# Attention and two expert layers on one core: the 1e-9 of the softmax sums added by a reduction over pairs instead of by a scalar addition

## Chip, cores and metric

The kernel runs on one core of a Trainium2 chip, as one launch. The metric is device microseconds of the whole execution, the median of the runs that were made of a kernel; lower is better.

## The reference

Three layers follow each other. The first is attention over 2 batches x 8 heads x 768 positions x 64 features, with a mask: every query and every key is assigned to the centroid (16 per head) that it is most similar to, and a query sees only keys of its own centroid.

```python
scores = np.where(mask, scale * np.matmul(q, k.transpose(0, 1, 3, 2)), -1e9)
attn = np.exp(scores - np.max(scores, axis=-1, keepdims=True))
attn = attn / (np.sum(attn, axis=-1, keepdims=True) + 1e-09)
out = np.matmul(attn, v)
```

The 1e-9 of the third line is what the change is about. The 1536 x 512 result then goes through a layer `s * relu(x @ w_in)**2 + b` times `w_out` (512 to 2048 to 512), and through eight experts of width 1024, whose gates are softmax values normalised eight times over rows and columns. All of it is float32.

## The kernel before

Float32 precision is had by splitting each float32 operand of a matrix product into a high part and a remainder (`hh`/`hl`, `ath`/`atl`, `xh`/`xl`, `wh`/`wl`) and multiplying the pairs of parts on TensorE.

**Attention** (the first fifth of the span) goes over 96 query tiles `g` (16 heads x 6 tiles of 128 queries); three tiles make a `half` (32 of them). For each tile TensorE makes 128 x 768 scores (`score`, L422), VectorE takes the negated row maximum from PSUM (`row_max`, `m`, L428), ScalarE takes the exponential and sums the row on the way (`expo`, L435, `accum_out` into one column of `sums`), TensorE transposes the result (`transp`, L450), ScalarE takes the transposed tile out of PSUM as `ath` (L457) and VectorE writes the remainder `atl` (L463), which frees the PSUM tile for the next transposes. TensorE then multiplies by the values (`values`, L473) while the next half is being made. Once per half VectorE adds 1e-9 to the three sums (`rsum`, L480) and takes their reciprocals (L481); TensorE broadcasts these over partitions (`rb_rows`, L487), ScalarE copies them out (`rs`, L497) and the output halves `xb`, `xt` (L499, L504), and GpSimd adds (L505) and scales (L506) the output into `x1`.

Other work is spread over the tiles by hand-written plans: the preparation of the next heads (`prepare`, `norms`), and, from tile 74 on, the first units of weights of the second layer. These are unpacked from words: ScalarE (L567, L569), VectorE (`bits`, L576, L578, L580), GpSimd (`join`, L587, L588), then a split into `wh` on ScalarE (L598) and `wl` on GpSimd (L600).

In attention the order of each engine's instructions is not that of the code alone: the framework orders them by priorities and its own estimates of time. The expert layers are inside `manual_schedule()`, where the order is that of the code. They begin with `x_parts(0)` on VectorE: four times a copy (L624) and a subtraction (L625), and TensorE's first products (L120) need these. The tiles `xh`, `xl` take the memory of attention's tiles, so the first L624 waits for the last L473. After that the rest of the span is one matrix product after another, with VectorE, ScalarE and GpSimd preparing the operands.

Of the kernel before, what the change touches and what calls it, by code (L numbers as in the profile page):

```python
# [8 lines left out]
F32 = mybir.dt.float32  # L9
# [5 lines left out]
AX = mybir.AxisListType  # L15
PSUM = bass.MemoryType.PSUM

P = 128
# [35 lines left out]
class Kernel:  # L54
# [69 lines left out]
    def constants(self):  # L124
        nc, per = self.nc, self.per
        cst = per.tile([P, 2 * P + 1], F32, name="cst")
        nc.sync.dma_start(cst, self.cst_in)
        self.ident, self.floor = cst[:, :P], cst[:, 2 * P : 2 * P + 1]

        self.band = per.tile([P, P], BF16, name="band")  # L130
        nc.vector.tensor_copy(self.band, cst[:, P : 2 * P])
# [209 lines left out]
    def attention(self):  # L341
        nc = self.nc
# [70 lines left out]
        sc, ex, sums, aT, pv = {}, {}, {}, {}, {}  # L413
# [16 lines left out]
        def expo(g):  # L430
            half, i3 = divmod(g, 3)
            if i3 == 0:
                sums[half] = self.tile("sums", [P, 3], bufs=3)
            e = ex[g] = self.tile("e", [P, S], bufs=2)
            nc.scalar.activation(  # L435
                e.rearrange("p (u k) -> p u k", u=2), sc.pop(g)[:, :, :HALF], AF.Exp,
                bias=sc.pop((g, "m")), accum_out=sums[half][:, i3 : i3 + 1],
            )

        def transp(g):  # L440
# [35 lines left out]
                    )  # L476

        def rsum(half):
            r = sums[half]
            nc.vector.tensor_scalar_add(r, r, 1e-9)  # L480
            nc.vector.reciprocal(r, r)  # L481

        def rb_rows(half):
            r = sums.pop(half)
            rb = pv[half, "rb"] = self.ps("t", [D, 512])
            for i in range(3):
                nc.tensor.transpose(  # L487
                    rb[:, i * P : i * P + P], r[:, i : i + 1].to_broadcast([P, D]), self.ident
                )
# [23 lines left out]
        row_max(0)  # L513
        score(1)
        expo(0)
        row_max(1)
        score(2)
        for g in range(n_tiles + 4):
            live = g < n_tiles
            if g + 2 < n_tiles:  # L520
                row_max(g + 2)
            if g + 1 < n_tiles:
                expo(g + 1)
            done = g // 3 - 1
            if g % 3 == 0 and done > 0:
                finish(done - 1)
            if live:
                ts = transp(g)
            if g + 3 < n_tiles:
                score(g + 3)  # L530
            if live:
                evac_hi(g, ts)
            if done >= 0 and g < n_tiles + 3:
                if g % 3 == 0:
                    rsum(done)
                values(done, g % 3)
                if g % 3 == 2:
                    rb_rows(done)
            for st in plan.get(g, ()):
                st[0](*st[1:])  # L540
            if live:
                evac_lo(g, ts)
            if g == 71:
                self.weights_follow()
                for u in range(3):
                    self.load_unit(u)
# [540 lines left out]
```

## Time and profile before

| | us |
|---|---|
| median of 3 runs | 1611.36 |
| lowest, highest | 1610.91, 1613.38 |
| profiled execution, device time | 1610.82 |
| its span, first to last instruction | 1609.0 |
| TensorE / VectorE / GpSimd / ScalarE busy | 1544.8 / 1009.2 / 892.3 / 766.4 |

The span is what the profile shows of the execution; 1.8 us of the device time lie around it. An engine that is busy with an instruction may be waiting inside it: the profile counts from the start of the instruction to its end. Times in the views count from the start of the span.

### The profile page before, as it was taken

To read this page: it belongs to the slowest core of one execution; us is meant where nothing else is said; L and a number is where in the kernel's file an instruction comes from. 1 tells how busy PE (TensorE), PEld (TensorE's weight loads), DVE (VectorE), ACT (ScalarE), POOL (GpSimd) and SP (SyncE) were. 2 spreads that over 40 slices of the span, in tenths; PEclk is the share of its full clock that TensorE was granted. 3 is DMA by queue.
4 is the path that set the end of the run, shared out by engine and by line. 5 is a ranking of instruction groups with operands and counts; after the bars stand their busy time and mean duration, and the time that the engine had idled before them with its cause. 6 is when DMAs were issued, how large, how long until landed. Compare 5 with 4: busy or idle time off the path is not lost.

```text
span 1609.0 us, 21766 instructions
## 1 busy us (share of the span) xinstructions
PE 1544.8 (96%) x8136; PEld 1402.2 (87%) x8136; DVE 1009.2 (63%) x1594; ACT 766.4 (48%) x1432; POOL 892.3 (55%) x650
## 2 busy tenths in 40 slices
PE   4899998799999999999999999999999999999998
PEld 3778996699999988889989988998899889889987
DVE  7999999787788475545445545565455455455454
ACT  4789899576656553343333333333343333333331
POOL 5664446423233556556666575668657565665652
PEclk7999999899999999999999999999999999999999
DMA  9774451112111002112112121213212121221211
GB/s 259 184 181 112 102 148 53 53 53 79 53 53 53 1 27 79 53 53 79 61 70 79 53 79 53 79 58 113 79 53 79 53 79 56 76 79 53 79 53 40
DMA packets 26793, 124.69 MB, mean 77 GB/s; under 512 B 4448, under 2 KB 4576, under 8 KB 16448
## 3 DMA queue, kind: packets, MB, share of 16 engines
q1 hardware_dynamic: 26112, 120.95, 23.5%
q0 software_dynamic: 576, 2.36, 0.7%
q8 instruction: 64, 1.05, 0.3%
q14 instruction: 41, 0.34, 0.1%
HBM read 99.80 MB, written 3.15 MB: 64 GB/s over the span
## 4 chain that ended last, share of the span: by engine, by line
PE 81%; DVE 9%; ACT 4%; issue 2%; DMA 2%; POOL 1%; SPq 0%; DVEq 0%; ACTq 0%; POOLq 0%
PE t L120 33%; PE s L938 22%; PE y L938 11%; PE s L664 6%; PE pv L473 3%; PE u L120 2%; PE s L422 2%; DVE atl L463 2%; DVE m L428 2%; PE t L450 1%; DVE sums L480 1%; ACT e L435 1%; DVE hl L650 1%; DVE c L852 1%; PE u L450 1%
## 5 line engine op out<-in xcount | busy, mean ns | idle before, releaser
L917 ACT ACTIVATE hh<-c 128x384 fp32r<-128x384 f32 x256 | 134.6, 526 | 619.7 <-PE y L938 250.2
L845 POOL TENSOR_TENSOR wl<-raw,wh 128x1024 fp32r<-128x1024 f32 x64 | 154.1, 2408 | 359.1 <-ACT wh L844 359.1
L918 DVE SCALAR_TENSOR_TENSOR hl<-c,hh 128x384 fp32r<-128x384 f32 x256 | 211.9, 829 | 170.9 <-ACT hh L917 170.9
L938 PE MATMUL s<-wh,hl 128*128 128x512 f32 x512 | 202.5, 396 | 0.0
L938 PE MATMUL s<-wl,hh 128*128 128x512 f32 x512 | 201.8, 394 | 0.0
L938 PE MATMUL s<-wh,hh 128*128 128x512 f32 x512 | 200.9, 392 | 0.0
L120 PE MATMUL t<-th,ah 128*128 128x384 f32 x512 | 173.2, 338 | 4.5 <-ACT c L977 1.9
L120 PE MATMUL t<-th,al 128*128 128x384 f32 x512 | 172.3, 337 | 0.0
L120 PE MATMUL t<-tl,ah 128*128 128x384 f32 x512 | 171.9, 336 | 0.0
L837 POOL TENSOR_TENSOR al<-sm,ah 128x1024 fp32r<-128x1024 f32 x64 | 165.7, 2589 | 4.9 <-ACT ah L834 4.9
L120 PE MATMUL t<-xh,ah 128*128 128x384 f32 x384 | 130.3, 339 | 0.1
L835 POOL TENSOR_TENSOR al<-raw,ah 128x768 fp32r<-128x768 f32 x64 | 129.7, 2027 | 0.0
L120 PE MATMUL t<-xh,al 128*128 128x384 f32 x384 | 129.7, 338 | 0.0
L120 PE MATMUL t<-xl,ah 128*128 128x384 f32 x384 | 129.3, 337 | 0.0
L988 DVE TENSOR_TENSOR c<-t,c 128x384 f32<-128x384 f32 x64 | 35.7, 558 | 142.8 <-PE t L120 142.8
L587 POOL TENSOR_TENSOR fa<-fa,wraw 128x1024 f32<-128x1024 f32 x16 | 39.1, 2445 | 148.9 <-ACT r L646 108.0
L938 PEld LDWEIGHTS s<-wh,hl 128*128 128x128 f32 x512 | 96.0, 187 | 22.1
L938 PEld LDWEIGHTS s<-wh,hh 128*128 128x128 f32 x512 | 96.1, 188 | 11.9
L938 PEld LDWEIGHTS s<-wl,hh 128*128 128x128 f32 x512 | 96.0, 188 | 11.8
L120 PEld LDWEIGHTS t<-th,ah 128*128 128x128 f32 x512 | 96.1, 188 | 10.2 <-ACT c L977 2.8
L938 PE MATMUL y<-wh,hl 128*128 128x512 f32 x256 | 100.8, 394 | 0.0
L938 PE MATMUL y<-wl,hh 128*128 128x512 f32 x256 | 100.7, 393 | 0.0
(219 smaller groups left out, 4067.9 us busy)
## 6 DMA issues: line engine op xcount, KB each, us to landing
raw<-in_w SPq DMA_DIRECT2D x64, 1024.0 KB, 4.8
wraw<-in_w SPq DMA_DIRECT2D x16, 1024.0 KB, 4.8
raw<-in_qk SPq DMA_DIRECT2D x16, 384.0 KB, 4.5
ka<-hi SPq DMA_DIRECT2D x28, 192.0 KB, 3.7
nat<-in_qkn SPq DMA_DIRECT2D x6, 768.0 KB, 6.5
vraw<-in_v SPq DMA_DIRECT2D x8, 384.0 KB, 4.8
out<-x SPq DMA_DIRECT2D x12, 256.0 KB, 2.1
qa<-hi SPq DMA_DIRECT2D x14, 192.0 KB, 2.6
```

The costliest lines, as they stand in the source:

```text
L120: self.nc.tensor.matmul(out, a, b, start=(i == 0), stop=(i == n - 1))
L422: nc.tensor.matmul(s[:, u, :HALF], a[:, qs], k[:, u * HALF : u * HALF + HALF], start=(a is qa), stop=(a is qb))
L473: nc.tensor.matmul(o, vt[:, kt].rearrange("p a d -> p (a d)"), aT[half][w][:, kt, :], start=(kt == 0 and w == 0), stop=(kt == QT - 1 and w ...
L587: nc.gpsimd.tensor_tensor(a, a, raw[:, :, 0].bitcast(F32), op=ALU.mult)
L664: nc.tensor.matmul(o, a, b, start=(start and i == 0), stop=(stop and i == 2))
L835: nc.gpsimd.tensor_tensor(al[:, : 3 * Q], raw[:, : 3 * Q], f32(ah[:, : 3 * Q]), op=ALU.subtract)
L837: nc.gpsimd.tensor_tensor(al[:, 3 * Q :], self.sums.rearrange("p a b -> p (a b)"), f32(ah[:, 3 * Q :]), op=ALU.subtract)
L845: nc.gpsimd.tensor_tensor(wl, raw[:, 1024:], f32(wh), op=ALU.subtract)
L917: nc.scalar.activation(hh, c, AF.Relu)
L918: nc.vector.scalar_tensor_tensor(hl, c, 0.0, f32(hh), op0=ALU.max, op1=ALU.subtract)
L938: nc.tensor.matmul(ys[t][m], a, b, start=(start and i == 0), stop=(stop and i == 2))
L988: nc.vector.tensor_tensor(p1, ta, p1, op=ALU.add)
```

## The change

Three tiles of [128, 3, 2] are made once and filled with 1e-9. ScalarE's running sums go into element 0 of each pair. In `rsum` a sum over the pairs (a TENSOR_REDUCE) takes the place of the addition of a constant (a TENSOR_SCALAR), and writes to a tile of its own, `rsum`, in which the reciprocal is then taken. The tile `sums`, of which there were three in turn, is gone.

```diff
         cst = per.tile([P, 2 * P + 1], F32, name="cst")
         nc.sync.dma_start(cst, self.cst_in)
         self.ident, self.floor = cst[:, :P], cst[:, 2 * P : 2 * P + 1]
+
+        self.sums3 = [per.tile([P, 3, 2], F32, name=f"sums{i}") for i in range(3)]
+        for t in self.sums3:
+            nc.vector.memset(t, 1e-9)
...
             if i3 == 0:
-                sums[half] = self.tile("sums", [P, 3], bufs=3)
+                sums[half] = self.sums3[half % 3]
...
-                bias=sc.pop((g, "m")), accum_out=sums[half][:, i3 : i3 + 1],
+                bias=sc.pop((g, "m")), accum_out=sums[half][:, i3, :1],
...
         def rsum(half):
-            r = sums[half]
-            nc.vector.tensor_scalar_add(r, r, 1e-9)
+            r = self.tile("rsum", [P, 3], bufs=2)
+            nc.vector.reduce_sum(r, sums[half], axis=AX.X)
             nc.vector.reciprocal(r, r)
+            sums[half] = r
```

## Rows read from the trace of the kernel before

**Rows 1.** The page's chain that ended last, shares of the span by engine.
```profile
PE 81%; DVE 9%; ACT 4%; issue 2%; DMA 2%; POOL 1%; SPq 0%; DVEq 0%; ACTq 0%; POOLq 0%
```
**Rows 2.** Stretches: length, each engine's busy time (instructions), clock, DMA share, GB/s.
```profile
core 0: us, PE busy (x) PEld busy (x) DVE busy (x) ACT busy (x) POOL busy (x), PEclk, DMA share, GB/s
...
294.00:301.00 7.00, 0.14 (x2) 0.07 (x2) 6.97 (x4) 1.53 (x4) 7.00 (x4) 0.70 0.42 150
301.00:307.00 6.00, 6.00 (x22) 5.55 (x22) 2.23 (x6) 1.43 (x4) 1.15 (x2) 0.50 0.00 0
307.00:312.00 5.00, 3.56 (x14) 2.23 (x14) 4.04 (x7) 0.99 (x3) 2.33 (x2) 1.00 0.00 0
312.00:400.00 88.00, 87.01 (x496) 86.60 (x496) 67.55 (x84) 62.24 (x112) 24.97 (x10) 1.00 0.17 58
```
**Rows 3.** TensorE's waits, 250 to 316 us: us in total, times, longest.
```profile
PE t L450 <- DVE atl L463: 13.7, 7, 6.9
```
**Rows 4.** The source view of line 480: ns minimum/median/maximum.
```profile
L480 DVE TENSOR_SCALAR sums<-sums x32: 147/160/6723, 45.4 to 293.5; 128x3 f32<-128x3 f32 x32
```
**Rows 5.** VectorE's groups of the whole span: busy us, mean ns | idle before.
```profile
L428 DVE TENSOR_REDUCE m<-s 128x1 f32<-128x768 f32 x96 | 90.8, 946 | 4.4 <-PE s L422 3.9
...
L480 DVE TENSOR_SCALAR sums<-sums 128x3 f32<-128x3 f32 x32 | 21.1, 658 | 1.4 <-ACT e L435 1.4
...
L212 DVE TENSOR_REDUCE rn<-nat 128x24 f32<-128x1536 f32 x4 | 7.0, 1738 | 1.1 <-ACT nat L197 1.1
...
L741 DVE TENSOR_REDUCE t<-pm 128x12 f32<-128x96 f32 x8 | 2.0, 252 | 0.0
```
**Rows 6.** Timeline of VectorE, 250 to 305 us: start, duration, instruction.
```profile
260.42 1.78 DVE L480 TENSOR_SCALAR sums<-sums 128x3 f32<-128x3 f32 x1
262.12 0.68 DVE L580 TENSOR_SCALAR fa<-ft 128x1024 uint32<-128x1024 uint32 x1
...
264.58 1.51 DVE L480 TENSOR_SCALAR sums<-sums 128x3 f32<-128x3 f32 x1
...
267.99 2.14 DVE L576 TENSOR_SCALAR ft<-fa 128x1024 uint32<-128x1024 uint32 x1
...
293.50 6.72 DVE L480 TENSOR_SCALAR sums<-sums 128x3 f32<-128x3 f32 x1 [1.19 <-ACT e L435]
```
**Rows 7.** Timeline of GpSimd, 250 to 305 us.
```profile
259.82 2.36 POOL L600 TENSOR_TENSOR wl<-ft,wh 128x1024 fp32r<-128x1024 f32 x1 [3.99 <-ACT wh L598]
...
266.14 1.00 POOL L506 TENSOR_TENSOR x<-xb,rs 64x384 f32<-64x384 f32 x1
...
293.22 2.38 POOL L587 TENSOR_TENSOR fa<-fa,wraw 128x1024 f32<-128x1024 f32 x1
...
297.86 2.33 POOL L588 TENSOR_TENSOR ft<-ft,fa 128x1024 f32<-128x1024 f32 x1
300.16 0.99 POOL L505 TENSOR_TENSOR xb<-xb,xt 64x384 f32<-64x384 f32 x1
```
**Rows 8.** Timeline of GpSimd, 620 to 640 us.
```profile
619.61 2.40 POOL L845 TENSOR_TENSOR wl<-raw,wh 128x1024 fp32r<-128x1024 f32 x1 [8.20 <-ACT wh L844]
```
**Rows 9.** Timeline of VectorE, the same stretch.
```profile
621.32 0.25 DVE L741 TENSOR_REDUCE t<-pm 128x12 f32<-128x96 f32 x1
```
**Rows 10.** Timeline of TensorE, 124 to 132 us.
```profile
129.50 0.55 PE L450 MATMUL t<-cst,e 128*128 128x128 f32 x3 [0.24 <-DVE atl L463]
```
**Rows 11.** ScalarE's waits, 250 to 296 us.
```profile
ACT ath L457 <- PE t L450: 3.6, 5, 1.0
```
**Rows 12.** The chain that ended last, 300 to 311 us, in order of time.
```profile
302.48 3.53 PE pv L473 x11
...
306.04 0.37 DVE xh L624
...
308.23 1.24 DVE xl L625
309.48 1.08 DVE xh L624
```
**Rows 13.** Timeline of VectorE at the kernel's start.
```profile
4.95 0.56 DVE L241 TENSOR_SCALAR raw<-raw 128x768 f32<-128x768 f32 x1 [1.31 <-DMA raw<-in_qk]
```

## The prediction

> **What bounds the kernel now.** I read the chain first. TensorE holds most of it, VectorE 9% [rows 1]. The table of stretches then says where TensorE is not full. From 312 us on it is busy 87 of 88 us [rows 2], and no wait there has to do with softmax, so the change can act on the expert layers only by letting them start earlier: whatever attention gains by its end, the whole time gains. From 294 to 301 us, on the other hand, TensorE is busy 0.14 us of 7, VectorE 6.97 and GpSimd all 7 [rows 2]. TensorE's list of waits names the reason: its transposes wait for VectorE's `atl`, 13.7 us between 250 and 316 us, and one of these waits is 6.9 us long [rows 3].
>
> The source view of L480 explains that wait. The addition takes 0.16 us in the median, but 6.72 us once [rows 4]. Its 32 executions sum to 21.1 us [rows 5], where 32 x 0.16 would be 5.1: 16.0 us of it are not work. Laid beside GpSimd's timeline, each long execution ends when a GpSimd instruction does: the one of 260.42 at 262.20, with L600's end at 262.18; the one of 293.50 at 300.22, with L588's at 300.19 [rows 6, 7]. VectorE is held by GpSimd inside this instruction. In the last case it is held through three GpSimd instructions in a row, from L587 at 293.22 to the end of L588 [rows 7], although two of them ended on the way.
>
> **What the change removes.** Does a TENSOR_REDUCE also wait for GpSimd? The nearest row is L741, a sum with source and destination in SBUF: 0.25 us from 621.32, while GpSimd's L845 ran from 619.61 to 622.01 [rows 8, 9]; it began and ended inside L845, at the mean of its eight [rows 5]. So I take it that the reduction does not wait. The Trainium skill says the same of this chip (SBUF — State Buffer, Who interferes with whom): an addition of a constant can use a port pair that VectorE shares with GpSimd, `tensor_reduce` never does.
>
> **What it adds.** Its own duration: 252 ns for 96 elements (L741) and 1738 ns for 1536 (L212) [rows 5] make 1.03 ns an element, so 6 elements cost 252 - 90 x 1.03 = 159 ns, the addition's median. Bounds: 147 ns, the shortest addition [rows 4], and L741's 252 ns, 0.09 more; six of the 32 lie where VectorE sets the pace (from 250 us), so 0.6 us at most. I take 159 and no difference. The three memsets run before VectorE idles 1.31 us for a load [rows 13]; even at 0.16 us each they are hidden, and without that cover they would cost 0.5 us. ScalarE writes the same sums at another step; no wait is added for it, because a tile of pairs comes back three halves later.
>
> **What of the 16.0 us lies on the path.** I go through the long executions.
>
> - Twelve executions are longer than 0.2 us. The six of them before 250 us hold 4.5 us of the stalls. TensorE is nearly full there. The longest of these (1.4 us, ending at 128.8) makes TensorE wait 0.24 us behind the `atl` that follows it [rows 10]. I take 0.2 us for all six; bounds 0 and 2.0 (1.2 if the whole of this one counts, and 0.8 at 45 us, where the chain names a DMA and not L480).
> - 260.42: the next VectorE instruction but for the reciprocal is L580, a TENSOR_SCALAR too, which then itself waits for L600 until 262.18 [rows 6, 7]. It ends where it ended. The same holds at 252, 281 and 285 us (L576, L576 and L578 come next). Gain 0.1, taken as 0.
> - 264.58: this one gains. It ends 1.35 us earlier, L576 (267.99) then comes at 266.6 and waits for L506 until 267.14 [rows 6, 7] instead of for L588, and ends at 267.7 in place of 270.13: 2.4 us earlier. But ScalarE stands in the same loop, and all it can give up from 250 to 296 us is 3.6 us of waits for TensorE's transposes, five of at most 1.0 [rows 11]; some 1.8 of these come by 276 us. I take 1.7, near that limit, because GpSimd's next instruction waits for ScalarE; bounds 0 and 2.4.
> - 293.50: without the stall, and with TensorE's clock still at 1.00 for the last L473s (11 in 3.53 us while 0.50 was granted, 1.2 of 2.4 GHz; at 1.00 the half of that, 1.8 us less [rows 2, 12]), L624 comes 6.56 + 1.8 = 8.3 us earlier, near 297.7 instead of 306.04.
>
> **Where the last stall goes.** L624 and L625 run with both operands in SBUF, and they wait for GpSimd too: L625 at 308.23 took 1.24 and L624 at 309.48 another 1.08 [rows 12]. At 297.7 GpSimd is still in its row of three. L624 will sit there until 300.19 [rows 7], as L480 did, and 2.4 us of the 8.3 are given back: 5.9 left. After that GpSimd has four more instructions of 1.0 us (L505 and L506 of the last two halves), of which two met the eight instructions before. All four may now alternate with them, or none: 5.9 - 2.1 = 3.8, or 5.9 + 1.5 = 7.4. I keep 5.9. Last the clock: it fell in the idle stretch of 294 to 301 us (mean 0.70), stood at 0.50 to 307 and was back at 1.00 [rows 2]. TensorE will now idle some 3 us and be half idle after that; a fall would cost at most the half of a stretch of 6 us, 3.0, and nothing where TensorE waits anyway. I take 1.0. So this place gives 4.9 us, with bounds 3.8 - 3.0 = 0.8 and 8.3 + 1.5 = 9.8.
>
> **The sum.** 0.2 + 1.7 + 4.9 = 6.8 us. The profiled execution had 1610.8 us, 0.5 below the median, so 1604.0 on it and 1604.5 for the median. Of the 16.0 us of stalls less than half comes back. The bounds add to 0.8 - 0.6 = 0.2 (1611.2) and 2.0 + 2.4 + 9.8 = 14.2 (1597.2).
>
> **Rivals.**
> 1. The wait only moves: L624 and L625 alternate with all four GpSimd instructions and the clock falls, so that under 3.2 us remain, 1609.5. For it: at four other places the next instruction takes the wait over. Against: GpSimd's work is the same and ends by about 304 us, so the row of eight must end before 311.
> 2. VectorE is let in at the end of each GpSimd instruction, and L624 runs at 297.9. Then nothing is given back: 0.2 + 1.7 + 9.8 = 11.7 us, 1599.7. Against: at 293.50 two ends passed without that [rows 6, 7]. The same section of the Trainium skill says that whoever starts first holds the pair for the whole instruction, from which one would expect VectorE in at 295.6; the 6.72 us disagree.
> 3. Slower: the framework orders attention's instructions by its own estimates. The code puts L481 right behind L480, yet L580 stands between them in time at 262.12 [rows 6], so the order is free to change with a new instruction and new tiles. If a maximum L428 (0.95 us [rows 5]) is put ahead of an `atl` for which TensorE waits, that costs 0.95 each; seven such halves of the 32 eat the 6.8 us, and at eleven it is 10.4 - 6.8 = 3.6 us slower, 1615.0. Against: operands, engine and undisturbed duration hardly change.
> 4. The change doesn't do what it says: a reduction over so small a tile waits for GpSimd like the addition. Then 1611.4. L741 speaks against it, with one instance inside a GpSimd instruction.
>
> **How the numbers follow.** Chances: the forecast (3.2 to 10 us gained, 1601.4 to 1608.2) 0.67; rival 1 0.11; rival 2 0.10; rival 3 0.07; rival 4 0.05. A measurement of this kernel can tell 0.2%, 3.2 us, from no change. Faster is the forecast and rival 2, 0.77; same rivals 1 and 4, 0.16; slower rival 3, 0.07. The range reaches from rival 2 with a little more, 1599, to rival 1, 1610, and leaves out rivals 3, 4 and the far end of the gains.
>
> **What would show it.** L480's line of reductions: all 32 near 0.16 us, none over 0.3. TensorE's wait of 6.9 us at 294 us gone; instead a wait of some 3 us for `xh` (L624), with a first L624 that takes over 2 us. L576 to L580 with as much waiting as before, apart from 268 us. TensorE's dense run beginning near 305 us in place of 312. I would be wrong if reductions of 1 us or more appear, if the order on VectorE differs in most halves, or if L624 gets in at once.

## The result and the profile after

| us | before | after |
|---|---|---|
| median (4 runs each) | 1611.13 | 1595.66 |
| lowest, highest | 1609.33, 1613.38 | 1594.16, 1598.94 |
| profiled execution, device time | 1610.82 | 1594.16 |
| its span | 1609.0 | 1592.4 |

The ratio is 0.9906 (95% 0.9886 to 0.9926): 15.5 us faster, with an interval of 11.9 to 18.4. Faster was forecast, but the forecast was 1604.5 and the range ended at 1599; the result lies 3.3 us outside it.

The lines of the kernel after count 4 or 5 higher (L480 is L484, L624 is L629, L938 is L943). First the source view of the reduction, the answer to [rows 4]: ns minimum, median, maximum, first and last start.

```profile
L484 DVE TENSOR_REDUCE rsum<-sums x32: 140/146/159, 44.5 to 287.3; 128x3 f32<-128x6 f32 x32
```

No reduction is held inside: 159 ns is the longest. The page's chain, which stood in [rows 1], has lost more than half of VectorE's share:

```profile
PE 85%; DVE 4%; ACT 4%; DMA 2%; issue 2%; POOL 1%; SPq 0%; ACTq 0%; DVEq 0%; POOLq 0%
```

VectorE's timeline (start, duration, instruction) from 256 to 301 us, shortened; it answers to [rows 6]:

```profile
256.41 0.14 DVE L484 TENSOR_REDUCE rsum<-sums 128x3 f32<-128x6 f32 x1
256.48 2.24 DVE L585 TENSOR_SCALAR fa<-ft 128x1024 uint32<-128x1024 uint32 x1
...
260.50 0.14 DVE L484 TENSOR_REDUCE rsum<-sums 128x3 f32<-128x6 f32 x1
...
262.67 0.95 DVE L581 TENSOR_SCALAR ft<-fa 128x1024 uint32<-128x1024 uint32 x1
...
287.25 0.16 DVE L484 TENSOR_REDUCE rsum<-sums 128x3 f32<-128x6 f32 x1 [1.19 <-ACT e L439]
...
291.63 2.52 DVE L629 CAST xh<-x 128x384 fp32r<-128x384 f32 x1 [1.33 <-PE pv L477]
294.26 1.16 DVE L630 TENSOR_TENSOR xl<-x,xh 128x384 fp32r<-128x384 f32 x1
295.34 1.15 DVE L629 CAST xh<-x 128x384 fp32r<-128x384 f32 x1
296.53 1.23 DVE L630 TENSOR_TENSOR xl<-x,xh 128x384 fp32r<-128x384 f32 x1
297.68 1.16 DVE L629 CAST xh<-x 128x384 fp32r<-128x384 f32 x1
298.88 0.56 DVE L630 TENSOR_TENSOR xl<-x,xh 128x384 fp32r<-128x384 f32 x1
299.35 0.35 DVE L629 CAST xh<-x 128x384 fp32r<-128x384 f32 x1
299.74 0.56 DVE L630 TENSOR_TENSOR xl<-x,xh 128x384 fp32r<-128x384 f32 x1
```

GpSimd's timeline of the end of attention, the answer to [rows 7]:

```profile
291.60 2.33 POOL L593 TENSOR_TENSOR ft<-ft,fa 128x1024 f32<-128x1024 f32 x1
293.90 1.10 POOL L510 TENSOR_TENSOR xb<-xb,xt 64x384 f32<-64x384 f32 x1
295.08 1.19 POOL L511 TENSOR_TENSOR x<-xb,rs 64x384 f32<-64x384 f32 x1
296.35 0.99 POOL L510 TENSOR_TENSOR xb<-xb,xt 64x384 f32<-64x384 f32 x1
297.42 1.21 POOL L511 TENSOR_TENSOR x<-xb,rs 64x384 f32<-64x384 f32 x1
```

And the table of stretches there, the answer to [rows 2] (columns as there):

```profile
295.00:301.00 6.00, 4.71 (x11) 2.95 (x12) 5.19 (x7) 0.47 (x1) 3.39 (x4) 0.55 0.00 0
301.00:306.00 5.00, 5.00 (x27) 5.00 (x26) 1.62 (x4) 3.58 (x7) 0.00 (x0) 0.86 0.02 3
306.00:400.00 94.00, 92.82 (x529) 92.05 (x528) 72.92 (x92) 64.58 (x116) 25.01 (x10) 1.00 0.16 57
```

At the end of attention the forecast can be followed instruction by instruction. L585 at 256.48 takes over the wait that the addition had at 260.42 before. The reduction at 260.50 ends where the addition of 264.58 stalled, and L581, at 262.67, has 0.95 us in place of 2.14. The last reduction takes 0.16 us. L629 then meets L593, started 0.03 us before it, and sits through it for 2.52 us. The granted clock averages 0.55 from 295 to 301 us (1.00 is 2.4 GHz, 0.50 is 1.2), and TensorE is full again from 301 us on.

All of that is attention. That it is not the whole is seen by lining up the same instructions of two traces and subtracting their starts. The following table is worked out in that way from the profiled executions (ScalarE's instructions, in order; times are those of the kernel before); each number is what a kernel gained on the kernel before *within* that stretch.

```
us of before   after   what lies there
   0 -  120    +3.19   loads, first heads
 120 -  140    +0.80   the stall of 127.40
 140 -  200    +0.05
 200 -  291    +2.21   the stall of 264.58
 291 -  399    +3.63   the last stall, x_parts, start of the expert layers
 399 -  700    +0.54
 700 - 1582    +6.15   expert layers
 sum          +16.57
```

The expert layers, where the diff changes no instruction, gained 6.15 us, and not by starting earlier. The table of stretches, cut at the same two instructions, first of before, then of after (length, then busy time and instructions of TensorE, its weight loads, VectorE, ScalarE and GpSimd, then the clock):

```profile
700.00:1582.00 882.00, 882.00 (x4393) 792.98 (x4392) 449.22 (x705) 308.49 (x528) 557.43 (x400) 1.00 0.19 68
```

```profile
689.58:1565.43 875.85, 875.85 (x4393) 792.90 (x4393) 412.92 (x705) 308.53 (x528) 559.33 (x400) 1.00 0.20 68
```

Both have 4393 recorded matrix products, TensorE busy without a gap, and the full clock; the stretch is 6.15 us shorter all the same. Some of the products have become a little quicker: of the second product's six groups four, by 2 to 5 ns, while the first product's (L120) kept theirs within 1 ns. Two of the four, first before, 700 to 1060 us, then after, in the stretch that answers to it (count | busy us, mean ns):

```profile
L938 PE MATMUL s<-wh,hl 128*128 128x512 f32 x185 | 73.2, 396 | 0.0
...
L938 PE MATMUL y<-wl,hh 128*128 128x512 f32 x92 | 36.2, 394 | 0.0
```

```profile
L943 PE MATMUL s<-wh,hl 128*128 128x512 f32 x185 | 72.4, 391 | 0.0
...
L943 PE MATMUL y<-wl,hh 128*128 128x512 f32 x93 | 36.2, 389 | 0.0
```

### The profile page after: what moved, and what is told of

Same layout as the page of the kernel before. It is cut to its first block, busy times and chain, and to the rows that moved or that the text cites. A ratio compares the mean times of both kernels' runs of the same rounds, so it can differ in the third digit from the quotient of the medians.

```text
span 1592.4 us, 21769 instructions
## 1 busy us (share of the span) xinstructions
PE 1538.0 (97%) x8136; PEld 1401.8 (88%) x8136; DVE 960.6 (60%) x1597; ACT 764.9 (48%) x1432; POOL 895.1 (56%) x650
## 4 chain that ended last, share of the span: by engine, by line
PE 85%; DVE 4%; ACT 4%; DMA 2%; issue 2%; POOL 1%; SPq 0%; ACTq 0%; DVEq 0%; POOLq 0%
PE t L120 34%; PE s L943 22%; PE y L943 11%; PE s L669 7%; PE pv L477 3%; PE s L426 2%; PE u L120 2%; PE t L454 2%; ACT e L439 1%; PE u L454 1%; DMA qa<-lo 1%; ACT ath L461 1%; DVE c L857 1%; DVE atl L467 1%; DVE m L432 0%
## 5 line engine op out<-in xcount | busy, mean ns | idle before, releaser
L923 DVE SCALAR_TENSOR_TENSOR hl<-c,hh 128x384 fp32r<-128x384 f32 x256 | 175.1, 685 | 176.7 <-ACT hh L922 176.7
L943 PE MATMUL s<-wl,hh 128*128 128x512 f32 x512 | 200.6, 392 | 0.0
L943 PE MATMUL s<-wh,hh 128*128 128x512 f32 x512 | 200.6, 392 | 0.0
L943 PE MATMUL s<-wh,hl 128*128 128x512 f32 x512 | 200.3, 391 | 0.0
L120 PE MATMUL t<-th,ah 128*128 128x384 f32 x512 | 173.2, 338 | 4.5 <-ACT c L982 1.9
L120 PE MATMUL t<-tl,ah 128*128 128x384 f32 x512 | 172.1, 336 | 0.0
L120 PE MATMUL t<-th,al 128*128 128x384 f32 x512 | 171.9, 336 | 0.0
L842 POOL TENSOR_TENSOR al<-sm,ah 128x1024 fp32r<-128x1024 f32 x64 | 157.1, 2454 | 4.2 <-ACT ah L839 4.2
L840 POOL TENSOR_TENSOR al<-raw,ah 128x768 fp32r<-128x768 f32 x64 | 137.9, 2154 | 0.0
L120 PE MATMUL t<-xh,ah 128*128 128x384 f32 x384 | 130.3, 339 | 0.1
L120 PE MATMUL t<-xh,al 128*128 128x384 f32 x384 | 129.5, 337 | 0.0
L120 PE MATMUL t<-xl,ah 128*128 128x384 f32 x384 | 128.8, 335 | 0.0
L592 POOL TENSOR_TENSOR fa<-fa,wraw 128x1024 f32<-128x1024 f32 x16 | 39.2, 2447 | 150.7 <-ACT r L651 107.9
L943 PEld LDWEIGHTS s<-wh,hl 128*128 128x128 f32 x512 | 96.1, 188 | 21.4
L943 PEld LDWEIGHTS s<-wh,hh 128*128 128x128 f32 x512 | 96.1, 188 | 11.5
L943 PEld LDWEIGHTS s<-wl,hh 128*128 128x128 f32 x512 | 96.2, 188 | 11.2
L120 PEld LDWEIGHTS t<-th,ah 128*128 128x128 f32 x512 | 96.2, 188 | 9.8 <-ACT c L982 2.8
L943 PE MATMUL y<-wh,hh 128*128 128x512 f32 x256 | 99.7, 390 | 0.0
L943 PE MATMUL y<-wh,hl 128*128 128x512 f32 x256 | 99.7, 390 | 0.0
```

What stands on the lines that cost most here:

```text
L120: self.nc.tensor.matmul(out, a, b, start=(i == 0), stop=(i == n - 1))
L592: nc.gpsimd.tensor_tensor(a, a, raw[:, :, 0].bitcast(F32), op=ALU.mult)
L840: nc.gpsimd.tensor_tensor(al[:, : 3 * Q], raw[:, : 3 * Q], f32(ah[:, : 3 * Q]), op=ALU.subtract)
L842: nc.gpsimd.tensor_tensor(al[:, 3 * Q :], self.sums.rearrange("p a b -> p (a b)"), f32(ah[:, 3 * Q :]), op=ALU.subtract)
L923: nc.vector.scalar_tensor_tensor(hl, c, 0.0, f32(hh), op0=ALU.max, op1=ALU.subtract)
L943: nc.tensor.matmul(ys[t][m], a, b, start=(start and i == 0), stop=(stop and i == 2))
```

## The experiments

The theory after the result (*two causes*): attention gave some 7 us, and the other 6 to 7 come from where things lie in memory. The diff takes the old `sums` out of attention's pool and puts three small tiles into the pool `per`, which is laid out first. In the memory plans of the two programs each of them takes 32 bytes of a partition, and the tiles allocated on that side behind them (`xh`, `hh`, `hl`, the expert layers' `wh` and `wl`, `x1`, ...) lie 96 bytes further on; `hh`, for one, at 93344 in place of 93248. Tiles of the other side (`th`, `tl`, `c`, `wraw`, ...) stay. The rival (*attention alone*): the expert layers gained for a reason that came with the reduction, such as a changed order or phase of the engines, and moving tiles alone does nothing.

### Tiles moved without the reduction, the reduction without moved tiles

The first kernel is the one before plus three unused tiles (**pad96**):

```diff
+        pads = [per.tile([P, 3, 2], F32, name=f"pad{i}") for i in range(3)]
+        for t in pads:
+            nc.vector.memset(t, 1e-9)
```

> The kernel before with three unused tiles of the size of the new pair tiles, made and filled at the same place: addition and order of instructions as before, but every tile on the left side of the memory lies 96 bytes higher, as after the change. Theory (two causes: about 10 us from the stalls in attention, about 6 us in the expert layers from the new addresses): 1604 to 1606 us; L480 still with executions over 1 us; from 600 us to the end about 983 us instead of 990. Rival (all of the gain is from the reduction): 1611 us, the expert layers as before.

The second is the kernel after with its pairs made in attention's pool, where `sums` had been, so that the expert layers' tiles lie as before (**unshifted**):

```diff
-        self.sums3 = [per.tile([P, 3, 2], F32, name=f"sums{i}") for i in range(3)]
-        for t in self.sums3:
-            nc.vector.memset(t, 1e-9)
+        self.sums3 = {}
...
+                if half < 3:
+                    self.sums3[half] = self.tile(f"sums{half}", [P, 3, 2])
+                    nc.vector.memset(self.sums3[half], 1e-9)
```

> The kernel after, with the three pair tiles made where the old sums lay, so that the tiles of the expert layers keep their addresses of before; reduction and order of instructions as after. Theory of two causes: 1601 to 1603 us, with the first dense products near 301 us as after, but the expert layers as slow as before. Rival (all from the reduction): 1595 to 1596 us, as after.

Measured: pad96 1605.44 us (12 runs), ratio 0.9959 (0.9948 to 0.9971), 6.6 us faster than before's 1612.09 of these sessions. Unshifted 1604.34 us (8 runs), ratio 0.9954 (0.9938 to 0.9970), 7.75 us faster. The two halves add to 14.4 us, inside the interval of the whole. The theory's 1604 to 1606 us for pad96 came true; its 1601 to 1603 us for unshifted was 1.3 us too low. The source view of pad96's addition shows that its stalls are all there:

```profile
L484 DVE TENSOR_SCALAR sums<-sums x32: 146/159/6709, 45.0 to 295.0; 128x3 f32<-128x3 f32 x32
```

and the table of stretches, cut at the same instructions as above, first pad96, then unshifted, that one has the short expert layers and the other the long ones, to 0.01 us:

```profile
700.39:1576.24 875.85, 875.85 (x4393) 792.87 (x4393) 412.90 (x705) 308.57 (x528) 559.26 (x400) 1.00 0.19 68
```

```profile
696.85:1578.85 882.00, 882.00 (x4393) 792.97 (x4392) 449.08 (x705) 308.48 (x528) 557.95 (x400) 1.00 0.19 68
```

So the reduction has no part in the expert layers' gain, and the tiles' place alone gives it. The rival falls. (The order of instructions is no rival either: pad96 has the order of before on every engine, but for its three memsets.) The gains by stretch, worked out as above:

```
us of before    after   pad96  unshifted  last_adds  join_later
   0 -  120     +3.19   -1.12    -3.95      +4.47      +1.03
 120 -  140     +0.80   -0.01    +0.77      +0.77      +0.80
 140 -  200     +0.05   -0.03    +0.07       0.00      +0.11
 200 -  291     +2.21   -0.30    +2.78      +2.79      +2.82
 291 -  399     +3.63   +0.31    +3.63      +0.54      +1.87
 399 -  700     +0.54   +0.76    -0.15      +0.52      +0.39
 700 - 1582     +6.15   +6.15     0.00      +6.16      +6.16
```

The first 120 us scatter by 4 us to either side: unshifted lost 3.95 there and after gained 3.19. A good part of that goes with TensorE's clock: the granted clock averaged 0.91 there in before, 0.94 in after, 0.93 in last_adds, 0.91 in join_later, and 0.90 in pad96 and unshifted, the two that lost. A single execution tells nothing of that stretch. The rows beneath it repeat better, but not to tenths: among the five kernels of this document that keep all additions with other places of the tiles (pad96 and four of the next section), 200 to 291 us came out between -0.95 and +0.71, and 291 to 399 us between -1.04 and +0.31.

One such difference can be named. Unshifted, last_adds and join_later gained some 0.6 us more than after between 200 and 291 us. All of it lies between 240 and 256 us, and pad96, without a reduction, gained 0.55 there too. The table of stretches, first of before, then of pad96, shows the granted clock (third number from the end):

```profile
240.00:255.00 15.00, 13.09 (x75) 11.90 (x74) 12.90 (x23) 13.81 (x31) 8.97 (x6) 0.89 0.20 72
```

```profile
240.00:255.00 15.00, 13.11 (x86) 11.79 (x85) 13.83 (x23) 14.54 (x34) 8.79 (x5) 1.00 0.14 49
```

In after it was 0.89 as well, and in unshifted, last_adds and join_later 1.00; in every other profiled kernel too the 0.6 us are there where the clock stayed at 1.00, and missing where it fell. So they are the clock's and not the reduction's.

### Which tile's place, and by what rule

If 96 bytes matter, which distances do, and whose? Single looks at seven other arrangements. Before plus one unused tile of 32 or 64 bytes (**pad32**, **pad64**), as in pad96 with `per.tile([P, 8], ...)` and `per.tile([P, 16], ...)`; after plus such a tile of 32, 64 or 128 bytes, which makes 128, 160 and 224 in all (**after_128**, which is shown, **after_160**, **after_224**):

```diff
+        pad = per.tile([P, 8], F32, name="pad")
+        nc.vector.memset(pad, 0.0)
```

And before with the operands of the second product moved apart: `wh` moved by 96 bytes and `hh`, `hl` left (**shift_w**), or `hh`, `hl` by 96 and `wh` by 128 (**shift_h**, with a first unused tile of 96 bytes ahead of `hh` and a second one of 32 bytes where shift_w has its own). The edit of shift_w:

```diff
+            if n == 0:
+                nc.gpsimd.memset(self.tile("pad", [P, 24]), 0.0)
```

> The kernel before with one unused tile of 32 bytes: all tiles on the left side lie 32 bytes higher (96 in the changed kernel). If any step off the old alignment helps: from 700 us to the end some 6 us less than before, as with 96 bytes. If the place modulo 64 decides: the same 6 us, since 96 and 32 are equal there. If it is the distance of 96 itself: another amount.

> The kernel before with one unused tile of 64 bytes. If the place modulo 64 decides: no gain in the expert layers, 0 us from 700 us to the end. If any shift helps: some 6 us. If there is a finer law of the address: something between, or a loss.

> The kernel before with an unused tile of 96 bytes placed so that only the tiles of the expert weights (wh, wl, the moving operand of L938) and what lies above them are shifted, while hh and hl (its stationary operand) stay. If the moving operand's address sets the pace of L938: 6 us less from 700 us to the end. If the stationary operand's address does: 0 us.

> The kernel before with hh and hl shifted by 96 bytes and the weights by 128. If the stationary operand's address sets the pace of L938: 6 us less from 700 us to the end. If the moving operand's does, and its place modulo 128 counts: 0 us.

> The kernel after with one more unused tile, so that the left side lies 128 bytes higher than before instead of 96. From 700 us to the end the shifts so far gained 0.6 (64 bytes), 1.3 (32) and 6.2 us (96) against the kernel before. If the gain is periodic with 128 bytes: 0 us there, 1601 to 1604 us in all. If it grows with the distance: 6 us or more.

> The same with 160 bytes. Periodic with 128: like 32 bytes, 1.3 us. Periodic with 64: like 96 bytes and like 32, which already differ, so this is not expected. No law of this kind: another amount, between a loss of 5 and a gain of 7 us.

> The same with 224 bytes. Periodic with 128: like 96 bytes, 6.2 us. Otherwise another amount, between a loss of 5 and a gain of 7 us.

Measured, with the gain from 700 to 1582 us, and the mean distance from one product's start to the next in the expert layers (ns, 128x512; worked out from TensorE's instructions in the traces):

```
              device us   700-1582   s: wl,hh to wh,hl   s: wh,hl to wh,hh   y: wh,hh to wl,hh
before                                    231.5               234.3               228.5
pad32           1612.93     +1.31         232.1               229.1               228.1
pad64           1610.59     +0.56         230.6               234.6               228.9
pad96           1605.44     +6.15         229.6               230.5               227.2
after           1595.66     +6.15         229.7               230.5               227.2
after_128       1599.98     +4.47         229.3               230.0               227.2
after_160       1603.49     +0.36         230.1               233.0               229.1
after_224       1597.52     +1.50         230.1               230.2               230.3
shift_w         1615.89     -5.26         234.4               234.7               233.8
shift_h         1616.04     -4.88         232.2               232.7               232.8
```

(One run each, except the medians of pad96 and after. The single runs of before beside them were 1612.09, and 1615.64 beside the three after_ kernels. The device times carry the scatter of the first 120 us, the middle columns don't.) The place of the operands moves this stretch of 882 us by 11.4 us from best to worst. The steps that the table leaves out changed too; the largest, from the last product of `s` to the first of `y`, went from 234.2 ns before to 227.4 after. In the trace of before, wherever the same two 128x512 products (the same parts of the same tiles) follow each other, 13 or 14 times each, the distance between their starts is the same to 1 ns, whatever the other engines do meanwhile; from one pair of places to another it goes from 224 to 241. So it is the place, and not a collision with other engines' work that comes at another time.

No rule of 32, 64 or 128 bytes fits: 128 gives 4.5, 160 nearly nothing, 96 gives 6.2. Nor is the distance between `wh` and `hh` the rule by itself: the seven kernels with tiles added in front (pad32 to after_224) keep it, and their gains go from 0.4 to 6.2; shift_w and shift_h change it, and cost 5.3 and 4.9, where 0 or 6 us less had been expected. What in the addresses sets the pace stays open.

### What the last stall was worth

To weigh that stall by itself, the kernel after with the addition back for the last half alone (**last_adds**):

```diff
-            nc.vector.reduce_sum(r, sums[half], axis=AX.X)
+            if half == 31:
+                nc.vector.tensor_scalar_add(r, sums[half][:, :, 0], 1e-9)
+            else:
+                nc.vector.reduce_sum(r, sums[half], axis=AX.X)
```

> The kernel after, with the addition of a constant put back for the last half alone. Theory (the last stall of 6.7 us is worth 4.6 us, the rest of it goes to the copies and subtractions that start the expert layers): 1600 us. Rival (it is worth all of its 6.6 us and the clock's 1.8 us): 1604 us. Other rival (earlier stalls carry the gain, the last one is hidden): 1596 us.

Measured: 1597.0 us (5 runs), ratio 0.9906 (0.9889 to 0.9923) against after's 1595.66. By its total the kernel can't be told from after. By its stretch it can: from 291 to 399 us it gained 0.54 us where after gained 3.63, so in the profiled executions this one instruction is worth 3.1 us; that of last_adds happened to have gained 4.47 us in the first 120. The theory, 4.6 us and 1600 us, was too high. VectorE's timeline of last_adds has the old stall again, through three GpSimd instructions:

```profile
285.47 6.62 DVE L485 TENSOR_SCALAR rsum<-sums 128x3 f32<-128x3 f32 x1 [1.19 <-ACT e L439]
...
297.47 0.36 DVE L632 CAST xh<-x 128x384 fp32r<-128x384 f32 x1 [2.65 <-PE pv L477]
```

and GpSimd's, with ends at 287.47, 289.77 and 292.07:

```profile
285.09 2.38 POOL L595 TENSOR_TENSOR fa<-fa,wraw 128x1024 f32<-128x1024 f32 x1
287.44 2.33 POOL L608 TENSOR_TENSOR wl<-ft,wh 128x1024 fp32r<-128x1024 f32 x1
289.74 2.33 POOL L596 TENSOR_TENSOR ft<-ft,fa 128x1024 f32<-128x1024 f32 x1
```

The Trainium skill (SBUF — State Buffer, Who interferes with whom) has the engine that starts first hold the shared pair for the whole instruction. L629's 2.52 us, through one GpSimd instruction, agree; the addition's 6.62 here, through the ends of two, do not, as the 6.72 of before did not.

### Can what is given back be kept?

The first L629 and four of the seven instructions behind it wait for GpSimd. Two ways around it. The copies on ScalarE (**xparts_act**):

```diff
-                if c:
+                if True:
                     nc.scalar.copy(xh[c][:, k], self.x1[c][:, k])
```

> The kernel after, with the four copies that start the expert layers on ScalarE, idle there, instead of VectorE. If the wait of 2.5 us at the first copy is on the path: 1592 to 1594 us, TensorE starts 2 us earlier. If the subtractions, which also read two operands from SBUF, take the wait over: 1595 to 1596 us.

Or GpSimd's two long instructions of the fourth unit held back until attention's last output is scaled (**join_later**; its core):

```diff
-                if u < EARLY or st[0] != self.split_unit:
+                if u < EARLY or st[0] not in (self.split_unit, self.join):
...
         x_parts(0)
+        self.join(EARLY)
```

> The kernel after, with GpSimd's two multiplications and additions of the fourth weight unit (join, L587 and L588 of before) pinned behind the last output of attention instead of ahead of it; addresses and the order on the other engines as after. If GpSimd's run of three instructions is what holds the first copy of the expert layers 2.5 us: that copy takes under 0.5 us, the dense products start 2 to 4 us earlier relative to the end of attention, 1592 to 1594 us. If the wait goes on to the copies and subtractions behind it: 1595 to 1596 us.

Measured: xparts_act 1596.53 us (6 runs), ratio 0.9902 (0.9880 to 0.9925); join_later 1597.13 (6 runs), ratio 0.9920 (0.9900 to 0.9939). Neither beats after. In xparts_act the wait goes to ScalarE and to the subtractions, and 3.9 us were gained from 291 to 399 us (TensorE's instructions lined up), 0.3 more than in after. Its chain that ended last, in order of time, goes through GpSimd's L592, L605, L593 and L510; the end of it:

```profile
297.05 2.37 POOL ft L593
299.42 0.96 POOL xb L510
300.38 0.02 issue
300.40 0.47 ACT xt L509
300.87 0.42 ACT xh L627
```

ScalarE's copy L509, ahead of L627 in its queue, waits for GpSimd's L510 there. VectorE's timeline has the four subtractions in one row:

```profile
301.32 3.58 DVE L630 TENSOR_TENSOR xl<-x,xh 128x384 fp32r<-128x384 f32 x4 [5.54 <-ACT xh L627]
```

which is 1.6 us more than the 1.96 that the next four took in after, with GpSimd idle. In join_later the first copies of its VectorE timeline are free, and the held-back pair catches the last ones:

```profile
293.11 0.36 DVE L631 CAST xh<-x 128x384 fp32r<-128x384 f32 x1 [1.32 <-PE pv L477]
...
297.26 2.54 DVE L631 CAST xh<-x 128x384 fp32r<-128x384 f32 x1
299.83 2.58 DVE L632 TENSOR_TENSOR xl<-x,xh 128x384 fp32r<-128x384 f32 x1
```

Its stretch from 291 to 399 us gained 1.87 us against after's 3.63. Some 0.6 us of that is the eight instructions, which took 9.3 us (293.11 to 302.41) in place of 8.67. The rest goes with the clock, which was still near 0.50 in join_later when it was back at 1.00 in after:

```profile
301.00:308.00 7.00, 5.53 (x18) 5.53 (x19) 2.46 (x3) 2.33 (x5) 1.00 (x1) 0.52 0.36 143
```

The wait can be placed, but neither place was free.

## Why the prediction was wrong

**The step that failed** is this one: "no wait there has to do with softmax, so the change can act on the expert layers only by letting them start earlier". The expert layers don't wait for softmax, which was right, but the change acts on them by the place of three new tiles. pad96 shows it: without any reduction, 6.15 us between 700 and 1582 us and 6.6 us in the median. In the sum this term was missing altogether; with unshifted, the kernel without it, the median is 1604.34, a gain of 7.75 where 6.8 was forecast. The new tiles had been weighed for their memsets alone, as time on VectorE, and never for the tiles that they move.

**The reduction doesn't wait, and the memsets cost nothing**: right. 140 to 159 ns were measured, 159 forecast. VectorE's timeline at the start has the memsets ahead of its first work, so VectorE's next wait for a load still covers them:

```profile
0.80 0.12 DVE L132 MEMSET sums<- 128x6 f32 x3 [0.80 <-PEq L1084]
...
5.19 0.56 DVE L245 TENSOR_SCALAR raw<-raw 128x768 f32<-128x768 f32 x1 [1.46 <-DMA raw<-in_qk]
```

**The stalls before 250 us**: 0.2 forecast, 0.8 measured from 120 us on, in all the kernels with reductions alike, and all of it from 120 to 140 us. What the two at 45 and 47 us were worth stays open, since they lie in the stretch that scatters. The chain that ended last, taken in that stretch of the kernel before, goes through that stall and on to TensorE, which [rows 10] with its wait of 0.24 us didn't let see:

```profile
126.38 1.00 ACT e L435 x2
127.38 0.02 issue
127.40 1.40 DVE sums L480
128.80 0.02 issue
128.82 0.17 DVE sums L481
129.00 0.46 DVE atl L463
129.45 0.04 issue
129.50 0.55 PE t L450 x3
```

A wait just behind a stall is not the stall's price. The bound of 1.2 for it was the better guide. What made up the rest of the price, behind the 0.24 us, was not measured.

**The stall of 264.58**: 1.7 forecast, 2.2 to 2.3 measured (256 to 276 us, in every kernel with reductions: after 2.22, unshifted 2.25, last_adds and join_later 2.26), close to the 2.4 by way of L576. The limit taken from ScalarE's waits [rows 11] was too tight. That nothing would be gained at 281 and 285 us was right (after, unshifted, last_adds and join_later stay within 0.05 us of nothing from 276 to 291 us), though at 281 us it is L428, and L576 only behind two `atl`, that comes next.

**The last stall**: 4.9 forecast, 3.6 measured. Of its parts, L629 came 14.41 us earlier, of which 6.25 were gained before: 8.2 earlier where 8.3 was forecast. It then took 2.52, against 0.37 before: 2.2 given back, 2.4 forecast. The size agrees in part by luck: L629 was to come 0.2 us before an end and sit past it, as the addition does, but it came within 0.01 us of L605's end and 0.03 us behind the start of L593, the last of the three, so that whether a copy passes an end was not put to the test. The eight instructions as a whole, from the first L629 to the end of the last L630, took 8.67 us (291.63 to 300.30), where before they took 5.1 (from 306.04 [rows 12] to 311.15, the last L625 being 0.57 us from 310.58); that gives back 3.6, so 1.4 beyond the first L629. This is the mis-sized part: "I keep 5.9" set the alternation with L510 and L511 at no more than before, while all four alternated; the text had worked out 2.1 for that case. The clock cost what was taken: 4.6 us were left at the end of the eight, 3.6 at 399 us, so 1.0. It was lost where TensorE's 128x384 products still followed each other after 0.32 us, up to 302.2 us, and after 0.17 to 0.18 us from there on.

So attention gave 0.8 + 2.2 + 3.6 = 6.6 us in the profiled execution of after and 7.2 in unshifted's, 0.6 of it the clock's at 246 us, for the 6.8 forecast. That this agrees is luck: the three terms, forecast less measured in after, were off by -0.6, -0.5 and +1.3 and cancelled out. With pad96's 6.6 this makes 13.2 to 13.8 of the 15.5 us; the rest is within the interval, and the scatter of the first 120 us doesn't let one look for it.

**The rivals.** Rival 1 (the wait only moves, under 3.2 us): wrong as a total, though its condition, the alternation with all four and the fall of the clock, came true; 3.6 us remained at that place. Rival 2 (VectorE let in at each end): its time, 1599.7, was nearer than the forecast, but for another reason: L629's 2.52 contradict that nothing is given back. Its mechanism is refuted for the addition alone, which passed two ends again in last_adds; the copies and subtractions got in after one instruction each. Rival 3 (a new order): on every engine the order stayed as it was, but for the three memsets and two of TensorE's products with `pv` that moved ahead of scores. Rival 4: no reduction over 0.16 us.

## What to carry to other kernels

A tile that is added, taken away or resized moves the tiles behind it, and on a kernel that is bound by TensorE this alone was worth from -5.3 to +6.2 us of 882. Build the control that moves the tiles and changes nothing else before crediting an edit, and compare the pace of stretches that the edit doesn't touch. A stall's price is read where its engine's chain goes on, not from the one wait behind it; and an instruction that ceases to wait for GpSimd can hand the wait to the next one of its engine that needs GpSimd to pause.

## What the runs showed of the hardware

- The pace of back-to-back matrix products depends on where their operands lie. With the full clock and no gap, 128x512 products followed each other after 226.7 to 235.8 ns in the mean, by kernel and pair of operands, and the same address gave the same pace in different kernels (before and unshifted, or after and pad96, agree to 0.02 us over 882).
- Waits for GpSimd can look like such an effect. `hl` on VectorE (L918, which reads two tiles in SBUF) took 818 ns in the mean before and 646 after in the stretches of the groups above, and 981 in shift_w. With no GpSimd instruction beside it, it took 0.54 to 0.56 us in all three; the mean goes with the waits for GpSimd. VectorE waits between them for ScalarE, 63.9 us in that stretch of before, and no effect of it on the total was seen.
- A small TENSOR_SCALAR was kept out through three GpSimd instructions in a row in all six other kernels that keep it (6.62 us in last_adds, 6.71 in pad96, up to 6.74), while copies and subtractions got in after one (1.15 to 1.36 behind the short ones, 1.88 to 2.59 behind the long ones).
- The first 120 us of the same instructions differ by up to 8.4 us between executions (from -3.95 to +4.47 against before), which is more than all of the sum's 6.8 us; the mean granted clock there went from 0.90 to 0.94.
